# Attention and a gated MLP on one core: where one batch's token combinations are made, and the order of GpSimd's steps in the gate phase

## Chip, core and metric

The kernel runs on one core of one Trainium2 chip. Its five engines are named as in the profile: PE (TensorE, with PEld for its weight loads), DVE (VectorE), ACT (ScalarE), POOL (GpSimd) and SP (SyncE, which here only issues DMAs). Each engine works through its own queue in order. The metric is the time of one execution on the device in microseconds (us); the time of a kernel is the median of its runs.

## What is computed

For 8 batches, 8 heads, 576 tokens and a head width of 64, a Nystrom attention with 32 landmarks, and on its output a gated MLP. Cut to what matters:

```python
A, Bm, C = sm(q, k_lm), sm(q_lm, k_lm), sm(q_lm, k)   # sm: scaled, softmax
Z = Bm.T / (norm1(Bm) * norminf(Bm))
for _ in range(6):
    Z = 2 * Z - Z @ Bm @ Z
x = (A @ Z @ C @ v)                 # [8*576 tokens, 512]
xn = x / rms(x) * rms_g
g, val = xn @ w_gate, xn @ w_val    # 512 -> 1536
out = (silu(g) * val) @ w_out       # 1536 -> 512, float32
```

## The kernel before

A batch's attention output is not written out as x. The kernel keeps AT, the transposed attention weights in front of the last small product, scaled by the norm, as an operand `an` of 2 x 128 rows and 576 tokens, split in a high and a low part; the small product is multiplied into the MLP's gate and value weights instead (matmuls `pM`, "mixing"). All large products run as three matmuls: high by high, high by low, low by high.

The hidden width of 1536 lies in twelve blocks f of 128, in six pairs. The **first pass** does pairs 0 to 2 for all batches: `mlp(early, b, ...)` (L470) mixes a pair's weights (`mix_weights`, DVE low part L281), makes `psg` and `psv` (gate and value), the silu on ACT (L503), the product by `psv` on DVE (L504, which also frees that bank), splits it (h, L509), and `outs` (L512) multiplies by the output weights into `pso`, five or four groups of 128 tokens per batch, two at a time. `keep` (L1102) copies each group on ACT to `ob` (L1104) and writes it to DRAM as a partial result `pd`. Interleaved with it runs the attention of the batches to come (`steady`, `rest(b)` L729, `second(b)` L932): transposes L663, Newton steps (L874 to L890), the scaling, and at its end the token combinations below. A mixer places this work by estimated times. Raw weights (`wraw`, later `lraw`) are loaded and split by ACT and DVE (L180 to L195) as they are needed.

The **second pass**, the gate phase `seven(b)` (L373) and its `outs` for each batch, does pairs 3 to 5 with seven block products in place of eight. It reads the batch's operand and its combinations from DRAM (`ad` to `xb`). The combinations t1 to t4 are made in the first pass by `token_blocks` (L994): a subtraction on DVE (`less`, L1000), an ACT cast (L1004), a low part on DVE (L1005) and two DMAs per combination (L1007). Three t tiles go round. Weight combinations are made by `mix_blocks` (L295): matmuls `pM` into two PSUM banks, sums S7 on DVE (L320 to L331), casts Bhi on ACT (L314 to L339), low parts on DVE, and the largest, Blo, on POOL (L344).

Per block f, `step(f, n)` issues product n as three matmuls `p` of 288 columns, and what belongs to it: copies u of a bank (ACT L425, DVE L429), sums vv (L432, L451) and s (L409), silu (L405 and in step 6), multiplies (DVE L412; `gate1`, POOL L406), and `split`: the cast h (ACT L416) and its low part (POOL L418). Two blocks' steps are woven: (f,1), (f-1,5), (f,2), (f,7), (f,6), (f-1,3), (f-1,4).

All these instructions stay in the order of the program text on their engines (`kept`). PSUM has four banks in a pool `pg` (psg, psv, pso, and some pM and p) and four in `pm`. The s tiles of the gate phase and S7 share a ring of four buffers, u and vv have two each.

Batch 0 differs: its combinations are made in `rest(1)`, one step of `token_blocks` behind each of batch 1's Newton steps, and its third pair (pair 5) is mixed in pieces by `between` within `seven(0)`, while the other batches have all three pairs mixed in the output stage before:

```python
next(blocks_of[b - 1], None)                  # rest(b), after each newton_step
def between(b, f):                            # called by seven(b, ...)
    if b == 0 and f == 1:
        pieces.append(mix_blocks(0, NPAIR + 2, (pg, "pg"), False))
```

Of the kernel before, what the change touches and what calls it, by code (L numbers as in the profile page):

```python
# [9 lines left out]
F32 = mybir.dt.float32  # L10
# [45 lines left out]
def nystrom_moe_kernel(  # L56
# [238 lines left out]
    def mix_blocks(b, pair, banks, whole_pair=True):  # L295

        ps = mixed_banks(late, b, pair, banks)

        def sums(whole=True):
            homes = HOMES[pair % NPAIR]  # L300
            hi = wp.tile([P, 7, 2, P], F32R, name="Bhi", tag=homes[0])
            if (b, pair) == (0, NPAIR + 1):
                lo1, lo2 = (mp.tile([P, n, 2, P], F32R, name=f"Blo{n}", tag="wraw", bufs=RAWS) for n in (3, 4))
            else:
                lo = wp.tile([P, 7, 2, P], F32R, name="Blo", tag=homes[1])
                lo1, lo2 = lo[:, :3], lo[:, 3:]
# [4 lines left out]
            blocks7[b, pair] = hi, lo1, lo2  # L311

            def high(n):
                kept(nc.scalar.copy(hi[:, n], (a11, a12, a22)[n]))  # L314

            def low(n):
                kept(nc.vector.tensor_sub(lo1[:, n], (a11, a12, a22)[n], hi[:, n].bitcast(F32)))

            kept(nc.scalar.copy(s[:, 2], a21))
            kept(nc.vector.tensor_add(s[:, 0], s[:, 2], a22))  # L320
            yield
            high(0)
            kept(nc.vector.tensor_sub(s[:, 1], s[:, 0], a11))
            yield
            kept(nc.vector.tensor_sub(s[:, 2], a11, s[:, 2]))
            if whole:
                kept(nc.scalar.copy(hi[:, 1:3], both[1]))
            else:
                high(1)
            yield  # L330
            kept(nc.vector.tensor_sub(s[:, 3], a12, s[:, 1]))  # L331
            if not whole:
                high(2)
            yield
            low(0)
            for n in (slice(0, 4),) if whole else (slice(0, 2), slice(2, 4)):
                if n.start:
                    yield
                kept(nc.scalar.copy(hi[:, 3 + n.start : 3 + n.stop], s[:, n]))  # L339
                if not whole:  # L340
                    low(1 + n.start // 2)
            if whole:
                kept(nc.vector.tensor_sub(lo1[:, 1:3], both[1], hi[:, 1:3].bitcast(F32)))
            silu["mix"] = kept(nc.gpsimd.tensor_sub(lo2, s, hi[:, 3:].bitcast(F32)))  # L344

        def at_once():
            for _ in sums():
                pass

        return at_once if whole_pair else sums(False)  # L350
# [13 lines left out]
    later, pieces = [], []  # L364
# [8 lines left out]
    def seven(b, xb, between):  # L373
# [4 lines left out]
        def product(f, n, ps, first):  # L378
            hi, lo1, lo2 = own[f]
            at, of = PRODUCTS[n]  # L380
            hi = hi[:, at, f % 2]
            lo = lo1[:, at, f % 2] if at < 3 else lo2[:, at - 3, f % 2]
# [19 lines left out]
        def gate1(f):  # L402
            s = ss[f]
            eng = nc.gpsimd if f < NF1 - 1 else nc.vector
            silu["last"] = kept(nc.scalar.activation(s[:, 1], banks[f][0], AF.Silu))  # L405
            kept(eng.tensor_mul(s[:, 1], s[:, 1], vv[f][:, 1]))  # L406
# [4 lines left out]
        def gate0(f):  # L411
            kept(nc.vector.tensor_mul(ss[f][:, 0], ss[f][:, 0], vv[f][:, 0]))  # L412

        def split(f):
            s, h = ss[f].rearrange("p e s -> p (e s)"), hs[f]
            kept(nc.scalar.copy(h[:, 0, TAIL:], s))  # L416
            eng = nc.gpsimd if f < NF1 - 1 else nc.vector
            kept(eng.tensor_sub(h[:, 1, TAIL:], s, h[:, 0, TAIL:].bitcast(F32)))  # L418

        def step(f, n):  # L420
# [3 lines left out]
            if n == 1:  # L424
                kept(nc.scalar.copy(u[:, 0], p1))  # L425
                if f > 1:
                    gate1(f - 2)
            elif n == 5:
                kept(nc.vector.tensor_copy(u[:, 2], p1))  # L429
                if f == 0:  # L430
                    first0(1)
                kept(nc.vector.tensor_add(v_[:, 1], u[:, 2], p7))  # L432
                if last:
                    gate1(f - 1)
                    gate0(f - 1)
                    split(f - 1)
            elif n == 2:
                if f != 1:
                    first0(f)
                if f > 1:  # L440
                    gate0(f - 2)
            elif n == 6:
                kept(nc.scalar.copy(u[:, 1], p1))
                kept(nc.scalar.activation(s[:, 0], s[:, 0], AF.Silu))
                if f > 1:
                    split(f - 2)
            elif n == 3:
                if last:
                    gate1(f)
            elif n == 4:  # L450
                kept(nc.vector.tensor_add(v_[:, 0], u[:, 1], p7))  # L451
                if last:
                    gate0(f)
                    split(f)
# [3 lines left out]
        for f in range(NF1):  # L458
            yield from between(f)
            new(f)  # L460
            second = ((1, 5), (0, 2)) if f > 1 else ((0, 2), (1, 5))
            for d, n in ((0, 1), *second, (0, 7), (0, 6), (1, 3), (1, 4)):
                if f >= d:
                    yield from step(f - d, n)
                if pieces and n in (7, 4):
                    next(pieces[0], None)
# [3 lines left out]
    def mlp(wts, b, f0, an, store, part, following):  # L470
# [39 lines left out]
        yield from outs(wts, b, f0, store, part, following, NF1 - 1)  # L510
# [37 lines left out]
    with tc.tile_pool(name="ap", bufs=1, side="right") as ap, tc.tile_pool(  # L548
# [180 lines left out]
        def rest(b, inverse, at):  # L729
# [27 lines left out]
            for n in range(6):  # L757
# [3 lines left out]
                next(blocks_of[b - 1], None)  # L761
# [13 lines left out]
            if b == B - 1:  # L775
                for _ in blocks_of[b]:
                    yield -0.3
# [154 lines left out]
        def second(b):  # L932
# [56 lines left out]
            blocks_of[b] = token_blocks(b, ATs, to)  # L989
            ans[b] = an  # L990

        blocks_of = {}

# [201 lines left out]
    def between(b, f):  # L1195
        if b == 0 and f == 1:
            pieces.append(mix_blocks(0, NPAIR + 2, (pg, "pg"), False))
            yield 1.1

    mix.fill(mlp(early, B - 1, 0, ans.pop(B - 1), keep, lambda t: None, first_blocks))  # L1200
    for b in range(B):
        mix.fill(seven(b, nxt["xb"], lambda f, b=b: between(b, f)))
# [41 lines left out]
```

## Time and profile before

| | |
|---|---|
| time, median of 3 runs | 820.45 us (818.88 to 821.15) |
| the profiled execution, its own time | 819.86 us |
| its span, first to last instruction | 818.1 us |
| instructions | 18012 |
| mean granted clock of TensorE | 0.985 of 2.4 GHz |
| DMA | 109.7 MB, mean 134 GB/s |

PE's busy digits in 40 slices of 20.5 us; 9 is 90% or more of a slice:

```profile
PE   7876999999999999999999998899999999999997
PEclk9888999999999999999999999999999999999999
```

The first five digits cover the loads and the attention of the first batches. The first pass ends and the gate phase of batch 0 starts at about 495 us; each later batch takes about 37 to 41 us, of which some 17 are its gate phase and the rest its output stage.

### The profile page before, as it was taken

Reading aid. Unit: us, or ns where it says so; the run is one execution under the profiler, and the core shown is the slowest. Engines: PE = TensorE matmul, PEld = TensorE weight load, DVE = VectorE, ACT = ScalarE, POOL = GpSimd, SP = SyncE. Lnnn points to the kernel's source line nnn. Section 1 sums busy time; section 2 is a strip of 40 time slices with the busy share of each in tenths; the row PEclk is TensorE's granted clock in tenths of the full one; section 3 lists DMA queues with packets and bytes.
Section 4 is the critical chain, followed back from the end, with each engine's and each line's share of the span. In section 5 each row is a group of like instructions: output and inputs, shape, how many; then the busy total and the mean of one; then the engine's idle time right before and its main releaser. Section 6 shows DMA issues by size and latency. Waiting matters only on the chain.

```text
span 818.1 us, 18012 instructions
## 1 busy us (share of the span) xinstructions
PE 782.2 (96%) x7012; PEld 623.8 (76%) x7012; DVE 598.0 (73%) x1360; ACT 418.1 (51%) x925; POOL 226.4 (28%) x234
## 2 busy tenths in 40 slices
PE   7876999999999999999999998899999999999997
PEld 5554667877778778777787877697979797979796
DVE  7999898758878858678586875767576656766662
ACT  4467645435455445454474955455354444545450
POOL 1004311020110200200101042555355535544550
PEclk9888999999999999999999999999999999999999
DMA  9846554352450541621548521233332424151512
GB/s 326 283 152 232 167 191 143 103 169 73 133 175 23 189 153 58 198 75 58 169 148 273 163 77 39 102 104 135 96 115 91 153 78 147 58 179 53 175 30 77
DMA packets 54629, 109.70 MB, mean 134 GB/s; under 512 B 5392, under 2 KB 28944, under 8 KB 54544
## 3 DMA queue, kind: packets, MB, share of 16 engines
q1 hardware_dynamic: 54544, 108.55, 39.8%
q8 instruction: 55, 0.90, 0.5%
q14 instruction: 30, 0.25, 0.1%
HBM read 73.14 MB, written 35.39 MB: 133 GB/s over the span
## 4 chain that ended last, share of the span: by engine, by line
PE 83%; DVE 8%; issue 3%; ACT 2%; DMA 2%; POOL 1%; SPq 0%; DVEq 0%; POOLq 0%; ACTq 0%
PE pso L111 36%; PE p L111 14%; PE psg L111 9%; PE psv L111 9%; PE pM L111 5%; PE pn L111 2%; PE sC L111 2%; PE pCV L111 1%; PE pss L111 1%; PE pO L111 1%; DMA qk<-in_k_dram 1%; DMA vl<-in_vl_dram 1%; PE sE L117 1%; PE pW L111 1%; DVE u L429 0%
## 5 line engine op out<-in xcount | busy, mean ns | idle before, releaser
L111 PE MATMUL pso<-wo,h 128*128 128x512 f32 x648 | 158.5, 396 | 0.8 <-DVE s L504 0.8
L111 PEld LDWEIGHTS pso<-wo,h 128*128 128x128 f32 x648 | 118.6, 188 | 32.4 <-ACT E L616 4.2
L111 PE MATMUL p<-xb,Bhi 128*128 128x288 f32 x672 | 139.2, 301 | 4.1 <-DVE s L409 1.6
L111 PE MATMUL pso<-lhio,h 128*128 128x512 f32 x432 | 140.6, 394 | 0.9 <-ACT h L416 0.6
L111 PEld LDWEIGHTS p<-xb,Bhi 128*128 128x128 f32 x672 | 109.2, 190 | 12.1 <-ACT u L425 2.8
L111 PE MATMUL p<-xb,Blo 128*128 128x288 f32 x336 | 99.6, 296 | 2.3 <-POOL Blo L344 2.3
L111 PEld LDWEIGHTS pso<-lhio,h 128*128 128x128 f32 x432 | 81.0, 188 | 25.3 <-issue 5.9
L111 PE MATMUL psv<-an,Mhi 128*128 128x288 f32 x384 | 84.4, 304 | 4.8 <-DVE s L504 4.8
L111 PE MATMUL psg<-an,Mhi 128*128 128x288 f32 x384 | 85.7, 307 | 2.1 <-ACT an L983 1.2
L111 PE MATMUL pso<-lloo,h 128*128 128x512 f32 x216 | 84.3, 390 | 0.0
L111 PEld LDWEIGHTS psg<-an,Mhi 128*128 128x128 f32 x384 | 62.4, 191 | 14.1 <-DVE WT L890 5.0
L344 POOL TENSOR_TENSOR Blo<-S,Bhi 128x1024 fp32r<-128x1024 f32 x24 | 57.6, 2399 | 53.8 <-ACT Bhi L339 53.8
L418 POOL TENSOR_TENSOR h<-s,h 128x576 fp32r<-128x576 f32 x40 | 58.7, 1468 | 41.2 <-ACT h L416 41.2
L111 PEld LDWEIGHTS psv<-an,Mhi 128*128 128x128 f32 x384 | 62.8, 191 | 7.6 <-DVE s L504 5.3
L111 PEld LDWEIGHTS p<-xb,Blo 128*128 128x128 f32 x336 | 63.6, 189 | 2.5 <-POOL Blo L344 2.5
L649 POOL TENSOR_TENSOR tA<-tA,mA 128x576 f32<-128x576 f32 x16 | 18.8, 1194 | 169.0 <-DVE mA L648 169.0
L503 ACT ACTIVATE s<-psg 128x288 f32<-128x288 f32 x96 | 39.3, 410 | 42.0 <-PE psg L111 41.3
L111 PE MATMUL psv<-an,Mlo 128*128 128x288 f32 x192 | 59.0, 308 | 0.0
L111 PE MATMUL psg<-an,Mlo 128*128 128x288 f32 x192 | 58.6, 305 | 0.0
L416 ACT CAST h<-s 128x576 fp32r<-128x576 f32 x48 | 32.2, 672 | 50.8 <-POOL s L406 27.9
L1104 ACT COPY ob<-pso 128x512 f32<-128x512 f32 x36 | 21.0, 589 | 72.2 <-PE pso L111 44.8
L1165 DVE TENSOR_TENSOR obl<-obl,pso 128x512 f32<-128x512 f32 x36 | 24.6, 684 | 40.6 <-PE pso L111 40.5
(170 smaller groups left out, 1529.3 us busy)
## 6 DMA issues: line engine op xcount, KB each, us to landing
xb<-ad SPq DMA_DIRECT2D x16, 1008.0 KB, 6.0
qk<-in_q_dram SPq DMA_DIRECT2D x16, 576.0 KB, 4.5
qk<-in_k_dram SPq DMA_DIRECT2D x16, 576.0 KB, 6.2
ad<-t SPq DMA_DIRECT2D x64, 144.0 KB, 2.1
pd<-ob SPq DMA_DIRECT2D x36, 256.0 KB, 3.5
obl<-pd SPq DMA_DIRECT2D x36, 256.0 KB, 2.8
out_dram<-obl SPq DMA_DIRECT2D x36, 256.0 KB, 2.1
vt<-in_v_dram SPq DMA_DIRECT2D x16, 512.0 KB, 5.5
```

What stands on the lines that cost most here:

```text
L111: tc.keep_in_program_order(nc.tensor.matmul(*args, **kw))
L117: tc.keep_in_program_order(nc.tensor.transpose(*args))
L344: silu["mix"] = kept(nc.gpsimd.tensor_sub(lo2, s, hi[:, 3:].bitcast(F32)))
L416: kept(nc.scalar.copy(h[:, 0, TAIL:], s))
L418: kept(eng.tensor_sub(h[:, 1, TAIL:], s, h[:, 0, TAIL:].bitcast(F32)))
L503: silu["last"] = nc.scalar.activation(s[:, cols], banks[0], AF.Silu).ins
L649: nc.gpsimd.tensor_sub(tA, tA, mA.unsqueeze(2).broadcast_to([P, NB, M]))
L1104: nc.scalar.copy(ob, ps)
L1165: kept(nc.vector.tensor_add(ob, ob, ps))
```

## The change

Three things are done.

1. Batch 0's token combinations are no longer made in `rest(1)`. Its two AT tiles are written to a new DRAM buffer, `x_dram`, and `first_x` reads them back at the end of `rest(7)`, where the combinations of batch 7 and then of batch 0 are made.
2. Batch 0's third pair is mixed by `first_blocks`, in the output stage of the last first-pass batch, together with the other two, which now begins after 8 group steps of three matmuls rather than 12. All late weights are loaded first. `homes_of` finds buffers for the blocks; the low part on POOL is two instructions there. `between` and the pieces go.
3. In the gate phase the silu of half 1 is issued in step 3 of its own block; POOL's multiply (`times1`) of f-2 stays in step 1, and the cast and POOL's subtraction (`split`) move from step 6, of f-2, to step 1 of the next block, of f-3. In the last block the order differs as written.

```diff
-    def seven(b, xb, between):
+    def seven(b, xb):
...
         def gate1(f):
-            s = ss[f]
-            eng = nc.gpsimd if f < NF1 - 1 else nc.vector
-            silu["last"] = kept(nc.scalar.activation(s[:, 1], banks[f][0], AF.Silu))
-            kept(eng.tensor_mul(s[:, 1], s[:, 1], vv[f][:, 1]))
+            silu["last"] = kept(nc.scalar.activation(ss[f][:, 1], banks[f][0], AF.Silu))
+
+        def times1(f, eng):
+            kept(eng.tensor_mul(ss[f][:, 1], ss[f][:, 1], vv[f][:, 1]))
...
             if n == 1:
                 kept(nc.scalar.copy(u[:, 0], p1))
                 if f > 1:
-                    gate1(f - 2)
+                    times1(f - 2, nc.gpsimd)
+                if f > 2:
+                    split(f - 3, nc.gpsimd)
...
                 if last:
-                    gate1(f - 1)
-                    gate0(f - 1)
-                    split(f - 1)
+                    times0(f - 1)
+                    times1(f - 1, nc.gpsimd)
+                    split(f - 2, nc.gpsimd)
+                    split(f - 1, nc.gpsimd)
...
             elif n == 6:
                 kept(nc.scalar.copy(u[:, 1], p1))
                 kept(nc.scalar.activation(s[:, 0], s[:, 0], AF.Silu))
-                if f > 1:
-                    split(f - 2)
             elif n == 3:
+                gate1(f)
                 if last:
-                    gate1(f)
+                    times1(f, nc.vector)
...
-    def mlp(wts, b, f0, an, store, part, following):
+    def mlp(wts, b, f0, an, store, part, following, after=2 * NF1):
...
-                next(blocks_of[b - 1], None)
+                if b > 1:
+                    next(blocks_of[b - 1], None)
...
             if b == B - 1:
-                for _ in blocks_of[b]:
-                    yield -0.3
+                first_x()
+                for late_b in (b, 0):
+                    for _ in blocks_of[late_b]:
+                        yield -1.0
...
-            blocks_of[b] = token_blocks(b, ATs, to)
+            if b:
+                blocks_of[b] = token_blocks(b, ATs, to)
+            else:
+                for g in range(2):
+                    nc.sync.dma_start(x_dram[:, g * S : (g + 1) * S], ATs[g])
...
+        def first_x():
+            xs = [ap.tile([P, S], F32, name="x0", tag="E", bufs=2) for g in range(2)]
+            for g in range(2):
+                nc.sync.dma_start(xs[g], x_dram[:, g * S : (g + 1) * S])
+            blocks_of[0] = token_blocks(0, xs, a_dram[0].rearrange("p (a n s) -> p a n s", a=2, n=7))
...
     def first_blocks():
         nxt["xb"] = load_x(0)
+        while late.order:
+            late.load_next()
         first = mix_blocks(0, NPAIR, (pm, "pm"))
         later.append(mix_blocks(0, NPAIR + 1, (pm, "pm")))
+        later.append(mix_blocks(0, NPAIR + 2, (pg, "pg")))
         first()
-        yield 2.0
+        yield 2.9
...
-    mix.fill(mlp(early, B - 1, 0, ans.pop(B - 1), keep, lambda t: None, first_blocks))
+    mix.fill(mlp(early, B - 1, 0, ans.pop(B - 1), keep, lambda t: None, first_blocks, 8))
```

The mixer sets the order of the queues, so three places are shown as they stand on an engine, before and then with the change.

DVE in the first pass, beside batch 1's Newton steps (t is a combination of batch 0, w a weight being split, s<-s,psv the product that frees a bank). Before:

```order
L185 SCALAR_TENSOR_TENSOR w_1044<-w_1044,wrawo_920 128x512
L1000 TENSOR_TENSOR t_1070<-AT 128x288
L663 STREAM_TRANSPOSE AT<-tA 128x576
L188 SCALAR_TENSOR_TENSOR w_1044<-wrawo_920,w_1044 128x512
L1000 TENSOR_TENSOR t_1072<-AT 128x288
L504 TENSOR_TENSOR s<-s,psv 128x288
L281 TENSOR_TENSOR Mlo<-pM,Mhi 128x512 x2
```

With the change:

```order
L185 SCALAR_TENSOR_TENSOR w_1047<-w_1047,wrawo_923 128x512
L504 TENSOR_TENSOR s<-s,psv 128x288
L663 STREAM_TRANSPOSE AT<-tA 128x576
L188 SCALAR_TENSOR_TENSOR w_1047<-wrawo_923,w_1047 128x512
L879 SCALAR_TENSOR_TENSOR PV<-PV,pn 128x192
L281 TENSOR_TENSOR Mlo<-pM,Mhi 128x512 x2
```

The two t are gone, and L504 stands where the first of them stood, ahead of the transpose and the second weight instruction.

ACT in the output stage of the first pass's last batch (lhio a late weight; S, Bhi or B... the blocks of a mixed pair; ob the copy that frees a pso bank). Before:

```order
L194 CAST lhio_6485<-w_6480 128x512
L1104 COPY ob<-pso 128x512 x2
L319 COPY S_6540<-pM 128x256
L314 CAST Bhi<-pM 128x256
L327 CAST Bhi<-pM 128x512
L339 CAST Bhi<-S_6540 128x1024
L1104 COPY ob<-pso 128x512
```

With the change:

```order
L194 CAST lhio_6492<-w_6487 128x512
L341 COPY S_6539<-pM 128x256
L332 CAST Bwgv_6537<-pM 128x256
L332 CAST Bwgv_6537<-pM 128x512
L332 CAST Bwgv_6537<-S_6539 128x1024
L1118 COPY ob<-pso 128x512
L341 COPY S_6566<-pM 128x256
```

The first ob copies stood ahead of the first pair's copies; now the first ob stands behind all four of them.

POOL in the gate phase of batch 1 (s<-s,vv is the multiply of half 1, h<-s,h the low part). Before:

```order
L406 TENSOR_TENSOR s_7073<-s_7073,vv 128x288
L418 TENSOR_TENSOR h_744<-s_7073,h_744 128x576
L406 TENSOR_TENSOR s_7095<-s_7095,vv 128x288
L418 TENSOR_TENSOR h_886<-s_7095,h_886 128x576
L406 TENSOR_TENSOR s_7129<-s_7129,vv 128x288
```

With the change:

```order
L408 TENSOR_TENSOR s_7082<-s_7082,vv 128x288
L408 TENSOR_TENSOR s_7104<-s_7104,vv 128x288
L419 TENSOR_TENSOR h_747<-s_7082,h_747 128x576
L408 TENSOR_TENSOR s_7139<-s_7139,vv 128x288
L419 TENSOR_TENSOR h_889<-s_7104,h_889 128x576
L408 TENSOR_TENSOR s_7176<-s_7176,vv 128x288
```

A block's subtraction followed its own multiply; now the multiply of the next block stands between them.

## Rows read from the trace of the kernel before

**Rows 1.** busy time of each engine over the span (the page's part 1)

```profile
PE 782.2 (96%) x7012; PEld 623.8 (76%) x7012; DVE 598.0 (73%) x1360; ACT 418.1 (51%) x925; POOL 226.4 (28%) x234
```

**Rows 2.** windows: length, busy PE, PEld, DVE, ACT, POOL, PEclk, DMA, GB/s

```profile
494.70:519.53 24.83, 19.98 (x138) 17.73 (x136) 14.28 (x31) 12.47 (x32) 11.60 (x9) 0.93 0.03 12
...
539.68:556.50 16.82, 16.59 (x121) 16.01 (x120) 12.40 (x26) 9.70 (x25) 8.26 (x11) 1.00 0.21 64
```

**Rows 3.** PE's waits by releaser, 480 to 818 us: sum, count, longest

```profile
PE p L111 <- POOL Blo L344: 2.3, 1, 2.3
...
PE p L111 <- ACT u L425: 1.1, 7, 0.2
```

**Rows 4.** timeline, DVE and PE, first pass: start, us, instruction, [idle before <-releaser]

```profile
75.28 0.53 DVE L1000 TENSOR_TENSOR t<-AT 128x288 f32<-128x288 f32 x1
76.86 0.78 DVE L663 STREAM_TRANSPOSE AT<-tA 128x576 f32<-128x576 f32 x1 [1.05 <-POOL tA L661]
...
78.50 0.45 DVE L504 TENSOR_TENSOR s<-s,psv 128x288 f32<-128x288 f32 x1
79.00 0.61 PE L111 MATMUL psv<-an,Mhi 128*128 128x288 f32 x1 [4.38 <-DVE s L504]
```

**Rows 5.** windows, as in group 2, of the stretch behind that wait

```profile
80.00:90.00 10.00, 9.99 (x115) 8.07 (x108) 7.39 (x16) 5.34 (x10) 2.23 (x3) 0.78 0.43 143
```

**Rows 6.** chain that ended last: start, us, engine, tile, line, matmuls

```profile
472.36 8.18 PE pso L111 x36
...
525.95 2.74 PE pM L111 x48
...
539.85 2.80 PE p L111 x21
```

**Rows 7.** timeline of ACT, outputs of the first pass's last batch

```profile
482.88 0.62 ACT L194 CAST lhio<-w 128x512 fp32r<-128x512 f32 x1 [1.95 <-DVE w L188]
...
484.37 0.39 ACT L319 COPY S<-pM 128x256 f32<-128x256 f32 x1
...
486.43 1.05 ACT L339 CAST Bhi<-S 128x1024 fp32r<-128x1024 f32 x1 [0.60 <-DVE S L331]
```

**Rows 8.** costliest groups (part 5): busy, mean ns | idle before, releaser

```profile
L1104 ACT COPY ob<-pso 128x512 f32<-128x512 f32 x36 | 21.0, 589 | 72.2 <-PE pso L111 44.8
```

**Rows 9.** timelines of POOL and DVE in gate phases 0 and 1

```profile
512.52 2.35 POOL L344 TENSOR_TENSOR Blo<-S,Bhi 128x1024 fp32r<-128x1024 f32 x1
513.31 1.88 DVE L412 TENSOR_TENSOR s<-s,vv 128x288 f32<-128x288 f32 x1
...
547.98 1.43 POOL L418 TENSOR_TENSOR h<-s,h 128x576 fp32r<-128x576 f32 x1 [1.22 <-ACT h L416]
549.38 0.80 POOL L406 TENSOR_TENSOR s<-s,vv 128x288 f32<-128x288 f32 x1
549.48 1.01 DVE L412 TENSOR_TENSOR s<-s,vv 128x288 f32<-128x288 f32 x1
```

**Rows 10.** timelines of ACT and PE, end of gate phase 1

```profile
553.79 0.68 ACT L416 CAST h<-s 128x576 fp32r<-128x576 f32 x1 [0.74 <-POOL s L406]
...
554.81 0.53 PE L111 MATMUL p<-xb,Bhi 128*128 128x288 f32 x2 [0.16 <-ACT u L425]
```

**Rows 11.** timelines of DVE and PE, last batch

```profile
796.35 1.48 DVE L406 TENSOR_TENSOR s<-s,vv 128x288 f32<-128x288 f32 x1 [3.10 <-ACT s L405]
...
799.45 0.50 PE L111 MATMUL pso<-lhio,h 128*128 128x512 f32 x1 [0.65 <-ACT h L416]
```

**Rows 12.** timelines of SP, ACT, DVE near the first pass's end

```profile
446.10 0.38 SPq L157 DMA_DIRECT2D wrawg<-in_moe_w_gate_dram  x1
...
449.47 1.27 ACT L1104 COPY ob<-pso 128x512 f32<-128x512 f32 x2 [5.02 <-issue]
...
451.79 1.29 DVE L281 TENSOR_TENSOR Mlo<-pM,Mhi 128x512 fp32r<-128x512 f32 x2 [5.75 <-ACT Mhi L279]
...
462.36 0.67 ACT L180 ACTIVATE wrawg<-wrawg 128x512 int32<-128x512 uint32 x1
```

More of the change, by code (lines that the diff above doesn't have):

```diff
@@ L293, in nystrom_moe_kernel, with homes_of, four, within @@
     blocks7 = {}
-    def mix_blocks(b, pair, banks, whole_pair=True):
-        ps = mixed_banks(late, b, pair, banks)
[L299 to L306, printed above, removed]
+    def homes_of(b, pair):
+        def four(pool, tag, bufs, n=2):
+            return pool.tile([P, n, 2, P], F32R, name=f"B{tag}", tag=tag, bufs=bufs)
+        names = HOMES[pair % NPAIR]
+        if b or pair == NPAIR:
+            hi, lo = (four(wp, n, 1, 7) for n in names)
+            return [(0, hi)], [(0, lo)]
+        if pair == NPAIR + 1:
+            lows = [(0, four(mp, "wraw", RAWS, 3)), (3, four(mp, "wraw", RAWS, 4))]
+            return [(0, four(wp, names[0], 1, 7))], lows
+        first = four(mp, "w32", WB)
+        highs = [(0, first[:, :1]), (1, four(mp, "w32", WB)), (3, four(mp, "wraw", RAWS, 4))]
+        lows = [(0, first[:, 1:]), (1, four(lp, "obl", 4)), (3, four(mp, "s", 2)), (5, four(mp, "s", 2))]
+        return highs, lows
+    def within(parts, a, z):
+        for at, t in parts:
+            lo, hi = max(a, at), min(z, at + t.shape[1])
+            if lo < hi:
+                yield lo, hi, t[:, lo - at : hi - at]
+    def mix_blocks(b, pair, banks):
+        ps = mixed_banks(late, b, pair, banks)
+        def sums():
+            highs, lows = homes_of(b, pair)
             s = lq.tile([P, 4, 2, P], F32, name="S7", tag="lraw", bufs=4)
@@ L310, in sums, with high, low @@
             a12, a22 = both[1][:, 0], both[1][:, 1]
[L311 to L317, printed above, removed]
+            source = {0: both[0], 1: both[1], 3: s}
+            def high(n, z):
+                for a, e, to in within(highs, n, z):
+                    kept(nc.scalar.copy(to, source[n][:, a - n : e - n]))
+            def low(n, z, eng):
+                (_, _, h), = within(highs, n, z)
+                for a, e, to in within(lows, n, z):
+                    silu["mix"] = kept(
+                        eng.tensor_sub(to, source[n][:, a - n : e - n], h[:, a - n : e - n].bitcast(F32))
+                    )
             kept(nc.scalar.copy(s[:, 2], a21))
             kept(nc.vector.tensor_add(s[:, 0], s[:, 2], a22))
-            yield
-            high(0)
+            high(0, 1)
             kept(nc.vector.tensor_sub(s[:, 1], s[:, 0], a11))
-            yield
             kept(nc.vector.tensor_sub(s[:, 2], a11, s[:, 2]))
[L326 to L330, printed above, removed]
-            kept(nc.vector.tensor_sub(s[:, 3], a12, s[:, 1]))
[L332 to L350, printed above, removed]
+            high(1, 3)
+            kept(nc.vector.tensor_sub(s[:, 3], a12, s[:, 1]))
+            low(0, 1, nc.vector)
+            high(3, 7)
+            low(1, 3, nc.vector)
+            low(3, 7, nc.gpsimd)
+            blocks7[b, pair] = highs, lows
+        return sums
     def load_x(b):
@@ L362, in behind @@
         return tc.issue_after(ins) if ins else nullcontext()
-    later, pieces = [], []
+    later = []
     hs, ends = [], []
@@ L378, in product @@
         def product(f, n, ps, first):
-            hi, lo1, lo2 = own[f]
             at, of = PRODUCTS[n]
-            hi = hi[:, at, f % 2]
-            lo = lo1[:, at, f % 2] if at < 3 else lo2[:, at - 3, f % 2]
+            hi, lo = (next(within(parts, at, at + 1))[2][:, 0, f % 2] for parts in own[f])
             for k, (w, x) in enumerate(((hi, xb[0]), (hi, xb[1]), (lo, xb[0]))):
@@ L440, in step @@
                 if f > 1:
-                    gate0(f - 2)
+                    times0(f - 2)
             elif n == 6:
@@ L452, in step @@
                 if last:
-                    gate0(f)
-                    split(f)
+                    times0(f)
+                    split(f, nc.vector)
             yield 3 * MMG
@@ L458, in seven @@
         for f in range(NF1):
-            yield from between(f)
             new(f)
@@ L509, in mlp @@
                 gated[b, f0 // NF1, 2 * n + i] = nc.vector.tensor_sub(h[:, 1, TAIL:], s, h[:, 0, TAIL:].bitcast(F32))
-        yield from outs(wts, b, f0, store, part, following, NF1 - 1)
+        yield from outs(wts, b, f0, store, part, following, NF1 - 1, after)
     def outs(wts, b, f0, store, part, following, n0, after=2 * NF1):
@@ L1193, in next_blocks @@
             yield 2.9
[L1195 to L1198, printed above, removed]
-    mix.fill(mlp(early, B - 1, 0, ans.pop(B - 1), keep, lambda t: None, first_blocks))
+    mix.fill(mlp(early, B - 1, 0, ans.pop(B - 1), keep, lambda t: None, first_blocks, 8))
     for b in range(B):
-        mix.fill(seven(b, nxt["xb"], lambda f, b=b: between(b, f)))
+        mix.fill(seven(b, nxt["xb"]))
         mix.fill(outs(late, b, NF1, finish, load_part, lambda b=b: next_blocks(b), NF1 - 2, 2 * NF1 - 4))
```

8 lines of the change are left out of this document (3 added, 5 removed).

## The prediction, made before the changed kernel was run

> **What bounds the kernel now.** I read the busy times first, then the chain that ended last, then the waits of PE by releaser, and the stretches on it one by one. PE is busy for 782.2 of 818.1 us [rows 1], so an edit pays where it takes away an idle stretch of PE, a stretch at the lower clock, or PE's own work; the change adds and removes no PE work but for its place. The profiled execution took 819.86 us around a span of 818.1; the median of the runs is 820.45, 0.6 above it. A measurement of this kernel tells 0.3%, some 2.5 us, from no change.
>
> Three places of PE loss lie where the diff reaches. The gate phase of batch 0 takes 24.83 us and that of batch 1, of the same products, 16.82 [rows 2]; the largest single wait in the second pass lies there, 2.3 us for POOL's low part of a weight combination [rows 3]. In the first pass PE waits 4.38 us at 74.6 to 79.0 for one DVE product that frees a bank [rows 4]. And the other gate phases run a little above their own pace: 21 matmuls take 2.80 us [rows 6], so the 120 of a gate phase would take 16.0, and it takes 16.82.
>
> **Part 1, batch 0's combinations leave the first pass.** On DVE's queue the psv product of L504 starts at 78.50. Ahead of it stand a subtraction t at 75.28, a transpose that waited 1.05 for POOL, a weight instruction and a second t [rows 4]. The row order of the change puts L504 where the first t stood: 78.50 - 75.28 = 3.22 us earlier, and PE's wait falls from 4.38 to about 1.2. The waits for the transpose and for the weights stay; they now stand behind the product that PE waits for. The clock: in 80 to 90 the granted clock is 0.78 of 2.4 GHz, a part of the stretch at 1.2, though PE is busy for 9.99 of 10 us there [rows 5]; it fell after the idle stretch. That cost up to 0.22 x 10 = 2.2 us and may come back. Eight DVE instructions of about 0.45 us less (3.6 us) also leave this stretch, where DVE sits between PE's steps. I take 3.2 + 1.3 = **4.5**; from below 1.5 (half of the 3.2 goes into the next waits, and the clock falls all the same), from above 5.4 (3.2 + 2.2).
>
> The same 8 DVE instructions, 4 ACT casts and 8 writes of 144 KB come back near the end of the pass (at about 442 to 450 us), with 2 writes and 2 reads of 288 KB through DRAM new. DVE has 5.75 us free before 451.79 and ACT 5.02 before 449.47 [rows 12]; added are 8 x 0.45 = 3.6 on DVE and 4 x about 0.4 = 1.6 on ACT (the 256-column copy of [rows 7] takes 0.39). That fits, with a rest of 2 us for waits on the t writes, since three t tiles go round. On SP's queue the first half of batch 0's operands, xb, is now issued behind these 8 writes, and the weight load of 446.10 behind it; what it feeds starts on ACT at 462.36 [rows 12], 16 us later, so a delay of 8 us is covered. Without the cover the wait lands on PE's outputs pso. I take **-0.3**, between 0 and -2. The two reloads stand on SP ahead of the first late weight load and wait for the last reader of their tiles; that weight load has the same 16-us kind of slack, and I cost it at nothing.
>
> **Part 2, the third pair is mixed early.** Gate phase 0 should now go at the pace of the others: 24.83 - 16.82 = 8.01 us [rows 2]. Its 16 mixing matmuls pM still run, now in the output stage before: 16 of 48 at 2.74 [rows 6] = 0.91. Net **+7.1**. Bounds: 5 (something of the waits returns, the POOL part being due for the third pair) to 7.1. POOL has three low parts of 2.35 us to make instead of two; they start near 487 and the last is due at about 494.7 + 4 x 2.8 = 506, so they are covered.
>
> But these 16 pM need two banks of the pool that pso uses. In the output stage of the last first-pass batch the order on PE is now 24 pso, 48 pM, 12 pso, and then the third group of pso needs the bank of the first. PE reaches it at 472.36 + 24 x 8.18/36 + 2.74 + 12 x 8.18/36 = 483.3 [rows 6]. The bank comes free with the copy ob of the first group, which in the change's ACT order stands behind the last weight cast lhio and the four casts of the first mixed pair. The weight cast ends at 482.88 + 0.62 = 483.50, and before the four took from 484.37 to 486.43 + 1.05 = 487.48 [rows 7]; the ob copies that stood between are gone from there, so the four start at 483.5 and end 0.9 earlier, at 486.6; an ob takes 0.59 [rows 8]. PE gets the bank near 487.2: a **new stall of 3.9 us**, ended by ACT ob. After a stall of this size the clock went to 0.78 once [rows 5], so I add 0.8: **-4.7**. Bounds 0 (the copy is let through earlier, or PE has other work there) and -6.
>
> **Part 3, the order of the gate phase.** The multiply of half 1 and the subtraction for h go on POOL one after the other at step 1, and the silu on ACT comes earlier. In the gate phase the last break of PE is its wait for ACT u at 554.81; ACT's queue was held by the cast of h, which waited 0.74 us for POOL's multiply [rows 10]. Such waits for u number 7 in the second pass [rows 3], one a batch. In the new order that cast comes an iteration later, when POOL's multiply is done. A gate phase loses 16.82 - 16.0 = 0.8; I take half for this break: 7 x 0.41 = 2.9, and half of the 0.65 that PE waits for h in the last batch, behind a DVE product that waited 3.10 for ACT's silu [rows 11]: 0.3. **+3.2**; bounds -4 (a new wait of 0.5 in each of 8 batches) and +5.6 (7 x 0.8).
>
> A row speaks against this part. DVE's multiply L412, both inputs in SBUF, takes 1.88 us beside POOL's low part Blo and 1.01 beside POOL's multiply [rows 9], against 0.45 for such a product alone [rows 4]. POOL's multiply and subtraction are now back to back: 0.80 + 1.43 = 2.2 of every 2.8 us [rows 9], so L412 will more often meet one. DVE is busy 12.40 of 16.82 us in a gate phase [rows 2], 2.07 per 2.80, so a single added block of 0.7 is still covered. The Trainium skill, SBUF — State Buffer, "Who interferes with whom", has a rule: a DVE instruction with two SBUF inputs and a GpSimd instruction that reads SBUF share a port pair as an exclusive lock, and the loser blocks for the whole instruction. By that rule L412 could wait for a whole subtraction in each iteration, which is rival C; the 1.88 and 1.01 above agree with it.
>
> **Sum.** 4.5 - 0.3 + 7.1 - 4.7 + 3.2 = 9.8. 819.86 - 9.8 = 810.1, with the runs' median 0.6 above the profiled execution: 810.5.
>
> **The rivals.**
> - A, no stall in the output stage (the bank is freed in time): 4.7 more, **805.8**. For it: PE's queue and ACT's differ by a few us only. Against: the ACT order of the change, in which ob stands behind four casts.
> - B, the first-pass gain is small because the next wait takes its place, 1.5 rather than 4.5: **813.5**. For it: the transpose that waited for POOL is still there [rows 4]. Together with part 3 at nothing and 2 us lost to the late combinations it would be 813.5 + 3.2 - 0.3 + 2 = **818.4**; I hold the half of that (816) likelier than the whole.
> - C, DVE becomes the bound of the gate phase: L412 blocked for a whole subtraction of 1.43 [rows 9] in each iteration. 2.07 + 1.43 = 3.50 us against 2.80, 0.7 for each of 5 iterations in 8 batches = 28: **838.5**, slower than before. It decides when DVE's time per iteration passes 2.80, so from a block of 0.73. Against: the longest in the rows is 1.88, and that beside an instruction of 2.35 us [rows 9]; the blocks of today already are inside the 12.40.
> - D, the change does not do what it says in batch 0: waits for the operands or for POOL's low parts keep gate phase 0 at 24 us, and the new stall comes on top: 810.5 + 7 = **817.5** to 820.
>
> **How the numbers follow.** The forecast has 0.50, A 0.13, B 0.22 (0.14 at about 813.5, 0.08 at 816 to 818.4), C 0.07, D 0.08. The forecast's own terms move it between about 807 and 814. The range reaches from 804.5 (A with a little more of the clock) to 816.5 (B with most of its additions) and leaves out C, D and the end of B. Faster by over 0.3% is everything below 818.0: the forecast, A, most of B and half of D, 0.87; within it the rest of B and D, 0.06; slower is C, 0.07.
>
> **What would show it.** First pass: the psv after 74.6 starts near 75.8 and the clock in 80 to 90 is near 1.00. Output stage: PE idle some 4 us near 483 to 487, ended by ACT ob. Gate phase 0 takes 17 us and no wait for POOL's low part is left. Later gate phases take 16.4 and the waits for ACT u are gone. Wrong would be: gate phases of 17 us or more with DVE L412 near 1.9 each (C), no stall near 483 (A), or a wait of PE near 450 to 462 for weights or for ob.

## The result

The changed kernel takes 812.17 us (median of 4 runs, 811.62 to 813.13) against 820.07 before (4 runs, 818.88 to 821.15): a ratio of 0.9905 with a 95% interval of 0.9887 to 0.9924, 7.9 us less. The forecast was 810.5 with a range of 804.5 to 816.5, so the time lies inside. Its terms did not come out so well: the first pass gave more than I took, and the new order of the gate phase costs where I had it gain.

The page of the changed kernel, its part 1, answers to [rows 1]; the span fell by 8.2 us:

```profile
span 809.9 us, 18024 instructions
PE 777.5 (96%) x7012; PEld 618.7 (76%) x7012; DVE 612.5 (76%) x1359; ACT 418.6 (52%) x923; POOL 226.5 (28%) x235
```

PE was busy 4.7 us less with as many matmuls; its mean granted clock rose from 0.985 to 0.992. DVE was busy 14.5 us more though it lost an instruction: its multiply in the gate phases takes longer, as shown below.

PE's waits of the changed kernel, 470 to 810 us (us in total, times, longest), answer to [rows 3]: the wait for POOL's low part is gone, one for ACT ob is new, and the wait for ACT u, 1.1 in 7 times before, has grown.

```profile
PE pso L111 <- ACT ob L1118: 3.5, 1, 3.5
PE p L111 <- ACT u L426: 1.8, 8, 0.2
```

The windows of the changed kernel (columns as in group 2): gate phases 0 and 1, the stretch after the first-pass wait, and the outputs behind the new stall.

```profile
493.33:510.37 17.04, 16.75 (x121) 16.03 (x121) 12.50 (x24) 10.46 (x27) 7.63 (x7) 1.00 0.05 17
530.71:547.68 16.97, 16.68 (x121) 16.02 (x121) 13.19 (x25) 9.97 (x26) 8.37 (x11) 1.00 0.21 63
...
78.60:88.60 10.00, 9.91 (x117) 8.10 (x116) 8.89 (x18) 7.59 (x16) 3.96 (x5) 1.00 0.43 155
479.29:493.33 14.04, 14.04 (x56) 11.47 (x57) 4.84 (x12) 5.83 (x11) 6.87 (x4) 0.89 0.37 131
```

Against [rows 2], gate phase 0 fell from 24.83 to 17.04 and gate phase 1 rose from 16.82 to 16.97. Against [rows 5], the clock of the first-pass stretch is 1.00 in place of 0.78.

**Where the 8.2 us lie.** Three pieces of the chain that ended last stand in both traces at the same place of the program, and cut the span into stretches. Of the changed kernel:

```profile
424.69 8.18 PE pso L111 x36
...
530.71 2.80 PE p L111 x21
...
766.93 2.80 PE p L111 x21
```

The same pieces before start at 432.46, 539.85 and 775.01:

```profile
432.46 8.18 PE pso L111 x36
...
775.01 2.80 PE p L111 x21
```

The first matmul `pss` of batch 0 (the sums of squares for the norm) marks the end of the start-up; it began at 38.24 before and at 36.74 with the change. The differences of these starts, and of the spans, give the table; the experiments are cut in the same way.

| kernel | to pss | first pass | outputs and gate phase 0 | six batches | rest |
|---|---|---|---|---|---|
| before | 38.24 | 394.22 | 107.39 | 235.16 | 43.09 |
| changed | 36.74 | 387.95 | 106.02 | 236.22 | 42.97 |
| e1_gate_only | 37.22 | 393.28 | 107.77 | 236.05 | 42.88 |
| e2_old_gate | 36.74 | 388.21 | 105.90 | 235.00 | 43.15 |
| e3_combos_only | 36.79 | 388.49 | 108.75 | 234.96 | 43.11 |
| e4_pair_only | 37.56 | 393.62 | 105.86 | 234.84 | 43.02 |
| e5_ob_first | 36.52 | 388.09 | 101.85 | 236.11 | 43.03 |
| e6_ob_first_old_gate | 37.04 | 388.27 | 101.67 | 234.80 | 43.22 |
| e7_split_at6 | 37.06 | 388.05 | 106.17 | 235.98 | 43.14 |
| e8_ob_first_split_at6 | 37.44 | 387.91 | 101.81 | 235.98 | 43.16 |
| e9_one_multiply | 37.43 | 387.86 | 101.44 | 233.20 | 42.17 |
| e10_three_u | 37.33 | 388.92 | 101.19 | 232.77 | 42.19 |
| e11_write_only | 37.10 | 388.51 | 101.00 | 230.92 | 41.27 |
| e12_one_multiply_three_u | 37.02 | 387.95 | 101.69 | 235.10 | 42.84 |

Of the 8.2 us, 1.5 lie in the start-up, where no edit acts: kernels with the same instructions there show 36.5 to 38.2, and from 30 us to the pss the granted clock was 0.80 before and 1.00 with the change. I take this for chance of single executions; with one trace of each kernel it is not shown. The edits gave 6.27 in the first pass and 1.37 around gate phase 0, and lost 1.06 in six later batches.

### The profile page after: what moved, and what is told of

It is laid out like the page before. It is cut to its first block, busy times and chain, and to the rows that moved or that the text cites. A ratio compares the mean times of both kernels' runs of the same rounds, so it can differ in the third digit from the quotient of the medians.

```text
span 809.9 us, 18024 instructions
## 1 busy us (share of the span) xinstructions
PE 777.5 (96%) x7012; PEld 618.7 (76%) x7012; DVE 612.5 (76%) x1359; ACT 418.6 (52%) x923; POOL 226.5 (28%) x235
## 4 chain that ended last, share of the span: by engine, by line
PE 77%; DVE 13%; issue 3%; ACT 3%; DMA 2%; POOL 1%; SPq 0%; DVEq 0%; ACTq 0%; POOLq 0%
PE pso L111 35%; PE p L111 10%; PE psg L111 9%; PE psv L111 9%; PE pM L111 5%; DVE s L414 3%; PE pn L111 2%; PE sC L111 2%; PE pCV L111 1%; DVE s L411 1%; PE pO L111 1%; DVE u L432 1%; DVE lmT L572 1%; PE pss L111 1%; PE sE L117 1%
## 5 line engine op out<-in xcount | busy, mean ns | idle before, releaser
L111 PE MATMUL pso<-wo,h 128*128 128x512 f32 x648 | 160.2, 399 | 3.5 <-ACT ob L1118 3.5
L111 PE MATMUL p<-xb,Bwgv 128*128 128x288 f32 x560 | 92.1, 297 | 0.5
L111 PEld LDWEIGHTS p<-xb,Bwgv 128*128 128x128 f32 x560 | 81.3, 188 | 3.0 <-DVE vv L435 2.4
L111 PE MATMUL p<-xb,Bwo 128*128 128x288 f32 x392 | 74.2, 300 | 1.6 <-ACT u L426 1.6
L111 PEld LDWEIGHTS p<-xb,Bwo 128*128 128x128 f32 x392 | 58.8, 188 | 7.6 <-ACT u L426 4.6
L408 POOL TENSOR_TENSOR s<-s,vv 128x288 f32<-128x288 f32 x40 | 36.8, 919 | 75.0 <-ACT s L405 55.5
L414 DVE TENSOR_TENSOR s<-s,vv 128x288 f32<-128x288 f32 x48 | 55.6, 1159 | 0.3
```

The costliest lines, as they stand in the source:

```text
L111: tc.keep_in_program_order(nc.tensor.matmul(*args, **kw))
L408: kept(eng.tensor_mul(ss[f][:, 1], ss[f][:, 1], vv[f][:, 1]))
```

## The experiments

My theory after these traces: part 1 gives some 6 us, part 2 gives 7.8 at gate phase 0 and gives most of it back in the stall, part 3 costs 1 us because DVE's multiply is held up beside POOL's subtraction. The rivals are that the later batches lose for another reason, and that the stall belongs to the moved weight loads.

**Each part alone (e1 to e4).** e1_gate_only is the kernel before with part 3 of the diff alone, as quoted ahead of the prediction. Expected:

> The kernel before with the new gate-phase order alone (part 3). Theory: POOL's subtraction now meets DVE's two-SBUF multiply L414 and blocks it, so each later gate phase is about 0.15 us longer than before: DVE multiply near 1.15 mean instead of 0.72, PE waits of 0.23 for ACT u stay, time 0.5 to 1.5 us above before (about 821). Rival: the order gains what was predicted (0.4 a batch, waits for ACT u gone) and the changed kernel loses its microsecond in the later batches elsewhere: about 817.

Measured 819.5 (10 runs, 818.42 to 820.70), ratio 0.9997 (0.9985 to 1.0009): no difference that the runs tell, and the rise of 0.5 to 1.5 that I expected does not show in them. The traces are sharper: six batches take 236.05 against 235.16, 0.9 us more, and the rest 0.2 less. The rival's gain of 3 us is excluded. DVE's multiply in the later gate phases (busy, mean ns | idle before) is the one instruction of DVE whose mean changed; first before, then in e1:

```profile
L412 DVE TENSOR_TENSOR s<-s,vv 128x288 f32<-128x288 f32 x42 | 30.1, 717 | 0.2
...
L412 DVE TENSOR_TENSOR s<-s,vv 128x288 f32<-128x288 f32 x42 | 49.0, 1167 | 0.2
```

e2_old_gate is the reverse, the changed kernel with the old order, in its core:

```diff
-                    times1(f - 2, nc.gpsimd)
-                if f > 2:
-                    split(f - 3, nc.gpsimd)
+                    gate1(f - 2)
...
+                if f > 1:
+                    split(f - 2)
```

> The changed kernel with the old gate-phase order (parts 1 and 2 only). Theory: about 1 us faster than the changed kernel, 811.2, with batch periods as in the kernel before (41.2 and 37.5 us) and the DVE multiply at 0.72. Rival: 3 us slower than the changed kernel, 815.

Measured 811.10 (810.78 to 811.17), 1.1 below the changed kernel; six batches take 235.00. The loss in the later batches comes with part 3 and goes with it: in the table every trace of the old order takes 234.8 to 235.2 for the six batches, and changed, e1, e5, e7 and e8, which have the early silu, take 236.0 to 236.2.

e3_combos_only puts part 1 alone on the kernel before (`x_dram`, `first_x`, and `if b > 1` in `rest`).

> The kernel before with part 1 alone (batch 0's combinations made at the end of the first pass). Theory: PE is 6 us ahead of before by 112 us (3.2 from the bank's wait, the rest from the clock behind it and from later waits of the same stretch) and keeps it: about 814. Rival: only the wait's 3.2 us are the change's, and the rest is chance of the start-up: 816.5 or later. Second rival: the late combinations delay the end of the pass by 1 us or more, seen as a new wait of PE between 430 and 495 us.

Measured 813.71 (812.91 to 814.69), ratio 0.9923 (0.9900 to 0.9945). The first pass takes 388.49 and keeps it. Between the 36 pso of the table and those of the last first-pass batch lie 465.17 - 425.28 = 39.89 us, before 472.36 - 432.46 = 39.90: the late combinations cost nothing.

```profile
425.28 8.18 PE pso L111 x36
...
465.17 8.18 PE pso L111 x36
```

e4_pair_only puts part 2 alone on the kernel before (`homes_of`, `first_blocks` with the third pair, `after` of 8, no `between`).

> The kernel before with part 2 alone (third pair mixed early, old gate order, combinations in the first pass). Theory: gate phase 0 is 7.8 us shorter, the output stage ahead of it 0.9 longer by pM and has a stall of 3.5 us that ends with ACT ob, with near 2 us at the lower clock behind it: net 1 to 2 us faster than before, about 818.7. Rival: the stall is made by the shift of the weight loads in part 1 and is absent here: about 813.

Measured 816.98 (10 runs, 816.43 to 818.59), ratio 0.9965 (0.9955 to 0.9976): 3 us faster, where the stretch of the table gives 1.5. The stall is there without part 1, so the rival falls:

```profile
PE pso L111 <- ACT ob L1102: 3.5, 1, 3.5
```

**The stall (e5, e6).** In e5_ob_first the sums of the first pair are issued behind the store of the first output group:

```diff
         later.append(mix_blocks(0, NPAIR + 2, (pg, "pg")))
-        first()
+        later.insert(0, first)
         yield 2.9
```

> The changed kernel with the first pair's sums issued behind the first ob copy of the last first-pass batch. Theory: the stall of 3.55 us is made by that copy standing behind the four casts, and the 1.6 us of lower clock behind it come from the stall: PE waits at most 0.6 there, the 54 pso after it take 12.5 instead of 14.0, and the time is 4.5 us below the changed kernel, 807.6. Rival: the blocks of the three pairs come later by as much, and gate phase 0 waits for POOL's low parts instead: about 811 to 812.

Measured 807.47 (807.23 to 809.34), 4.7 below the changed kernel. In the changed kernel's timelines of ACT and PE (start, us, instruction, idle before and releaser) the first ob stands last, and PE starts when it is done; this answers to [rows 7]:

```profile
475.13 0.62 ACT L194 CAST lhio<-w 128x512 fp32r<-128x512 f32 x1 [1.95 <-DVE w L188]
475.66 0.37 ACT L341 COPY S<-pM 128x256 f32<-128x256 f32 x1
...
477.70 1.04 ACT L332 CAST Bwgv<-S 128x1024 fp32r<-128x1024 f32 x1 [0.60 <-DVE S L347]
478.66 0.58 ACT L1118 COPY ob<-pso 128x512 f32<-128x512 f32 x1
...
479.29 2.93 PE L111 MATMUL pso<-wo,h 128*128 128x512 f32 x6 [3.55 <-ACT ob L1118]
```

In e5_ob_first the ob follows the weight cast at once and PE waits 0.55; in the window behind it the clock is 1.00 where it was 0.89. The timelines:

```profile
475.05 0.62 ACT L194 CAST lhio<-w 128x512 fp32r<-128x512 f32 x1 [1.95 <-DVE w L188]
475.58 0.58 ACT L1118 COPY ob<-pso 128x512 f32<-128x512 f32 x1
...
476.21 0.96 PE L111 MATMUL pso<-wo,h 128*128 128x512 f32 x3 [0.55 <-ACT ob L1118]
```

and the window of its next 56 pso:

```profile
476.21:489.08 12.87, 12.83 (x56) 10.32 (x57) 7.35 (x18) 7.83 (x15) 6.89 (x5) 1.00 0.34 115
```

So the order on ACT makes the stall, and without the stall the clock did not fall: 3.55 - 0.55 = 3.0 us of waiting and 14.04 - 12.87 = 1.2 in the pace of the pso behind it are the 4.2 by which the stretch of the table shrank. Gate phase 0 did not come to wait for POOL.

e6_ob_first_old_gate adds the old gate order of e2_old_gate.

> The kernel of e5_ob_first with the old gate-phase order too. Theory: the losses of the stall and of the new gate order add, so 1 us below e5_ob_first: about 806.6. Rival: the new gate order only costs what chance of the start-up shows, and the two are equal within 0.3 us; the batch periods tell it (41.2 and 37.1 against 41.4 and 37.3 us).

Measured 807.34 (806.37 to 808.37): equal to e5_ob_first within the runs, where 1 us was expected. Its trace has the 1.3 us in the six batches (234.80 against 236.11), less 0.2 at the end and 0.5 of a later start-up; the runs alone don't settle it. Of three pairs that differ in part 3 alone (before and e1, e2 and changed, e6 and e5), all traces show its loss of 0.9 to 1.3 in the six batches, and the runs of one pair do, by 1.1.

**Why the gate order costs (e7 to e12).** One block of the changed kernel's gate phase 1, in the timelines of POOL, DVE, ACT and PE:

```profile
543.15 1.43 POOL L419 TENSOR_TENSOR h<-s,h 128x576 fp32r<-128x576 f32 x1 [0.86 <-ACT h L418]
543.20 1.70 DVE L414 TENSOR_TENSOR s<-s,vv 128x288 f32<-128x288 f32 x1
...
544.82 0.44 DVE L454 TENSOR_TENSOR vv<-u,p 128x288 f32<-128x288 f32 x1
...
545.38 0.40 ACT L426 COPY u<-p 128x288 f32<-128x288 f32 x1 [1.08 <-DVE vv L454]
...
545.83 0.40 PE L111 MATMUL p<-xb,Bwo 128*128 128x288 f32 x1 [0.23 <-ACT u L426]
```

DVE's multiply starts 0.05 us after POOL's subtraction and takes 1.70, near the 1.43 of the subtraction and its own 0.45 after it. DVE's next sum vv is late by as much, ACT's copy u waits 1.08 for vv, and PE waits for u. Over the 42 such copies of the later batches ACT's idle time that vv ended rose from 6.7 us before to 19.4 with the change:

```profile
L425 ACT COPY u<-p 128x288 f32<-128x288 f32 x42 | 16.6, 395 | 44.6 <-PE p L111 37.6 <-DVE vv L451 6.7
...
L426 ACT COPY u<-p 128x288 f32<-128x288 f32 x42 | 16.7, 399 | 57.9 <-PE p L111 38.5 <-DVE vv L454 19.4
```

e7_split_at6 moves the subtraction away, on the changed kernel:

```diff
             if n == 1:
...
                 if f > 1:
                     times1(f - 2, nc.gpsimd)
-                if f > 2:
-                    split(f - 3, nc.gpsimd)
...
                     times1(f - 1, nc.gpsimd)
-                    split(f - 2, nc.gpsimd)
                     split(f - 1, nc.gpsimd)
...
             elif n == 6:
...
+                if f > 1:
+                    split(f - 2, nc.gpsimd)
```

> The changed kernel with the cast of h and POOL's subtraction back at step 6 of f-2, the silu kept early. Theory: what blocks DVE's multiply L414 is the subtraction issued at step 1 beside it; moved away, the multiply falls from 1.16 to 0.75 mean or less, and since the silu is early the cast no longer waits for POOL, so the waits for ACT u (0.23 each) go below 0.1: gate phase 16.5, time 2 to 4 us below the changed kernel, 808 to 810. Rival: the early silu itself shifts ACT's copies u, and the gate phase stays at 17.0: 812.

Measured 812.61 (811.77 to 813.17): the rival. The multiply's mean fell to 827 ns, yet the six batches take 235.98. In its ACT timeline the cast of h waits for POOL's multiply again, and now the early silu too stands ahead of u, for which PE waits 1.7 us in 9 times after 490 us:

```profile
545.21 0.67 ACT L418 CAST h<-s 128x576 fp32r<-128x576 f32 x1 [0.42 <-POOL s L408]
545.79 0.40 ACT L405 ACTIVATE s<-p 128x288 f32<-128x288 f32 x1
546.10 0.39 ACT L426 COPY u<-p 128x288 f32<-128x288 f32 x1
```

So u can be late by ACT's order as well as by DVE, and the two orders only trade one for the other. e8_ob_first_split_at6 has the edits of e5 and e7.

> The kernels of e5_ob_first and e7_split_at6 together. Theory: both gains add: about 804 to 805.5. Rival: the ring of buffers or DVE becomes the limit when both are in, and the gain is only that of e5_ob_first: 807.6.

Measured 808.09 (807.89 to 808.32): the gain of e5_ob_first alone, as e7 lets one think.

e11_write_only tests, on e5_ob_first, whether it is POOL's reading that holds up the multiply:

```diff
-            kept(eng.tensor_sub(h[:, 1, TAIL:], s, h[:, 0, TAIL:].bitcast(F32)))
+            if eng is nc.gpsimd:
+                for _ in range(2):
+                    kept(eng.memset(h[:, 1, TAIL:].bitcast(F32), 0.0))
+            else:
+                kept(eng.tensor_sub(h[:, 1, TAIL:], s, h[:, 0, TAIL:].bitcast(F32)))
```

> The kernel of e5_ob_first with POOL's subtraction replaced by two writes of zeros over the same tile: the low part of h is left out for blocks 0 to 4 of each gate phase. Theory: DVE's multiply L414 is blocked by POOL instructions that read SBUF; beside writes alone it stays near 0.45, its mean falls from 1.16 to 0.7 or less (the multiply on POOL is left), and PE's waits for ACT u fall below 0.1. Rival: POOL's being busy at all, or the order of L414 among its neighbours, makes it long: the mean stays above 1.0.

One run, 800.62. POOL is still busy with 70 writes, and the multiply takes its own time:

```profile
L414 DVE TENSOR_TENSOR s<-s,vv 128x288 f32<-128x288 f32 x42 | 19.0, 453 | 0.2
...
L421 POOL MEMSET h<- 128x576 f32 x70 | 40.1, 579 | 2.0
...
535.29 1.22 POOL L421 MEMSET h<- 128x576 f32 x2
536.25 0.45 DVE L414 TENSOR_TENSOR s<-s,vv 128x288 f32<-128x288 f32 x1
```

The writes start earlier than the subtraction did, and in this block the multiply meets only their last 0.26 us; held up until they end, at 536.51, it would have taken some 0.7, an estimate from these two rows, and it took 0.45. The waits for u are gone and six batches take 230.92, 5.2 less than in e5_ob_first. So it is POOL's reading, not its being busy, that makes the multiply long. The Trainium skill, SBUF — State Buffer, "Who interferes with whom", says that a DVE instruction with two SBUF inputs contends with a GpSimd instruction that reads SBUF and not with one that only writes it; 1.70 us beside the subtraction and 453 ns beside the writes agree.

e9_one_multiply takes POOL's multiply away, on e5_ob_first:

```diff
+        def times(f):
+            kept(nc.vector.tensor_mul(ss[f], ss[f], vv[f]))
...
             if n == 1:
...
-                if f > 1:
-                    times1(f - 2, nc.gpsimd)
-                if f > 2:
-                    split(f - 3, nc.gpsimd)
...
                 if f > 1:
-                    times0(f - 2)
+                    times(f - 2)
...
             elif n == 6:
...
+                if f > 1:
+                    split(f - 2, nc.gpsimd)
```

> The kernel of e5_ob_first, both halves multiplied in one DVE instruction of 576 columns at step 2, and cast and POOL's subtraction at step 6 of f-2. POOL's multiply is gone from blocks 0 to 4, so the subtraction is over before the next DVE multiply. Theory: that multiply takes 0.8 (no block) in place of 1.16 + POOL's 0.92, the cast no longer waits, and PE's waits for ACT u fall below 0.1 each: 2 to 4 us below e5_ob_first, 803.5 to 805.5. Rival: ACT's order (cast and silu ahead of u, as in e7_split_at6) holds u back by itself: 807 or more.

Measured 803.85 (803.67 to 803.89), ratio to the kernel before 0.9804 (0.9787 to 0.9822), 3.6 below e5_ob_first. The multiply of 576 columns takes 1034 ns, not the 0.8 expected, but the trace's list of PE's waits has none for u any more.

```profile
L417 DVE TENSOR_TENSOR s<-s,vv 128x576 f32<-128x576 f32 x35 | 36.2, 1034 | 0.0
```

e10_three_u keeps the changed gate order of e5_ob_first and has a third buffer for u:

```diff
-            us[f] = mp.tile([P, 3, HS], F32, name="u", tag="Mhi", bufs=2)
+            us[f] = (lp.tile([P, 3, HS], F32, name="u", tag="u3", bufs=1) if f % 3 == 2
+                     else mp.tile([P, 3, HS], F32, name="u", tag="Mhi", bufs=2))
```

> The kernel of e5_ob_first with three buffers for u in place of two. Theory: ACT's copy u of a block waits for DVE's sum vv of the block two before because it takes that block's u buffer; with a third this wait goes, but a blocked DVE still reaches PE by the banks, so 0.1 to 0.3 us a gate phase come back: 805.5 to 807. Rival: the wait moves to DVE vv in full, and the time stays at 807.5.

Measured 803.55 (803.14 to 804.14), ratio 0.9802 (0.9787 to 0.9818): 3.9 below e5_ob_first, where I had given it 0.5 to 2. The multiply still takes 953 ns on average and PE no longer feels it. Its chain runs 90 products without a break, 12.20 us where e9 needs 12.56:

```profile
531.50 12.20 PE p L111 x90
...
552.80 15.52 PE pso L111 x66
```

So the wait for u was a wait for its buffer: the block lengthens DVE's work, and only the ring of two hands that on to PE.

e12_one_multiply_three_u has both edits.

> The kernels of e9_one_multiply and e10_three_u together. Theory: e9 still ran its 90 matmuls p in 12.6 us where e10 ran them in 12.19, and e10 lost 0.37 us a batch in the output stage, where e9 did not; with both, 12.2 and the shorter output stage: 0.43 x 8 = 3.4 us below e9_one_multiply, about 800.5. Rival: with POOL's multiply on DVE the sum vv is late for the banks all the same, and it stays between 802.5 and 804.

Measured 806.69 (5 runs, 806.35 to 808.18): slower than either, and neither theory gave it. Its 90 products take 12.57, as in e9. ACT's queue there has the cast, the silu and u back to back, without a wait (540.11 to 541.38), so I take ACT's order for the limit of both, which a buffer more doesn't help; no run moves that order alone. And its outputs are slower than in e9:

```profile
530.73 12.57 PE p L111 x90
...
552.38 15.52 PE pso L111 x66
```

Of e9_one_multiply the same pieces, with 15.22 for 66 pso:

```profile
530.87 12.56 PE p L111 x90
...
552.44 15.22 PE pso L111 x66
```

## Why the prediction held, and where it did not

**Part 1 was too small in its size: 4.5 forecast, 6.3 measured in the profiled pair, 5.5 as the mean of the three first passes with the old place of the combinations (393.7) less that of the others (388.2).** The step went as written: L504 starts at 73.87 and PE waits 1.16, of the forecast 1.2.

```profile
73.87 0.43 DVE L504 TENSOR_TENSOR s<-s,psv 128x288 f32<-128x288 f32 x1
...
74.36 0.40 PE L111 MATMUL psv<-an,Mhi 128*128 128x288 f32 x1 [1.16 <-DVE s L504]
```

The term was mis-sized twice. I counted 1.3 us for the clock, and 1.8 came back: the work from 79.00 to 84.23, at a granted clock of 0.50, took 5.23 us before, and the same work with the change 3.99, of which 0.56 is a new wait (columns as in group 2; first before, then with the change).

```profile
79.00:84.23 5.23, 5.23 (x44) 4.15 (x45) 3.46 (x8) 1.83 (x4) 1.21 (x1) 0.50 0.47 157
...
74.36:78.35 3.99, 3.36 (x45) 2.45 (x45) 3.11 (x7) 1.24 (x3) 1.87 (x2) 1.00 0.21 25
```

And two more waits of PE for L504 lay in the stretch, which I had read past; before, the waits from 60 to 113 us contain

```profile
PE psv L111 <- DVE s L504: 4.8, 2, 4.4
...
PE pso L111 <- DVE s L504: 0.8, 1, 0.8
```

which are 5.6 us for the one releaser, and 1.2 with the change. New waits of 0.6, 0.7 and 0.3 us (for the attention tiles PV, sqT and sq) took 1.6 of that back: 4.4 - 1.6 + 1.8 = 4.6. The other 1.7 of the profiled pair's 6.3 I can't place. The two other kernels with the old code (e1, e4) have a longest wait of 3.6 and 3.7 there rather than 4.4 and are 0.6 to 0.9 faster in the first pass, so a part of it is that execution's.

**The late combinations: -0.3 forecast, 0.0 measured** (e3). No new wait shows, so the room on DVE and ACT [rows 12] was enough.

**Part 2 was right in its mechanism and near in its sizes.** Gate phase 0 fell by 7.8 us where 8.0 was forecast, and mixing costs what was worked out. The stall came at the place, by the releaser and at the size written down, 3.55 against 3.9; the clock behind it cost more than the 0.8 that I took: the 54 pso took 14.04 us, against 12.87 in e5 and 12.46 before. Net +2.4 forecast, 1.4 in the profiled pair and 1.5 from before to e4. From e3 to e2 it is 2.9: in e3 the longest wait of gate phase 0 was followed by the lower clock, which cost 1.5 us there and did not happen before (the last section has the rows). So the profiled pair shows the least of what part 2 is worth.

**Part 3 failed: +3.2 forecast, -0.9 measured.** The step that failed is "in the new order that cast comes an iteration later, when POOL's multiply is done", from which I took half of the gate phase's loss. The cast no longer waited; but u is released by the later of two, ACT's queue and the buffer that DVE's vv frees, and the new order made the second later. Rival C was the right mechanism with the wrong price. It put 0.7 us on PE in each of five blocks. In gate phase 1 the multiplies take 1.28, 1.70, 1.70 and 1.38, which is 0.8 to 1.25 over the 0.45 of one alone, and DVE's period reaches 546.47 - 543.20 = 3.27 us by the starts of L414 in two blocks. But PE's 90 products took only 0.16 more, 12.91 (534.77 to 547.68) against 12.75 before (543.91 to 556.66), since the rings of buffers take up the first delays. The gain itself was to be had: without the wait for the buffer they take 12.20 in e10. The view that I should have followed one step further is the chain behind [rows 10]: I stopped at the first releaser of u and did not ask what is late next.

So the sum, 9.8 against 7.9 of the medians, came near by terms that failed in both directions: 1.0 to 1.8 too little in part 1, 0.3 of loss that did not come, and 4.1 too much in part 3; part 2 was between 1.0 too much and 0.5 too little. That the time lies so near the forecast is in part luck.

## What to carry to other kernels

When a change moves an instruction past a wait, list every resource that the waiting instruction needs (its queue, its operand, its output buffer) and compute when each comes free in the new order; the last one decides. An instruction that frees a PSUM bank belongs ahead of work that nobody waits for on its queue: one line moved took away 3.0 us of a 3.55-us stall and the lower clock behind it. And a DVE multiply with both inputs in SBUF is better kept away from POOL instructions that read SBUF, or given a buffer more to take up the delay: e9_one_multiply and e10_three_u, at 803.9 and 803.6, beat both kernels. The two together, in e12, do not add.

## What the runs showed of the hardware that I had not expected

In e10 and e12 every pso of the second pass is some 2% slower than in e9 and e5: 66 take 15.52 us in place of 15.22, 48 take 11.34 or 11.35 in place of 11.14, at the same count and a granted clock of 1.00 in the windows of all four, and the matmuls pso of the first pass take 8.18 for 36 in all of them. What the two kernels share is the third u buffer in the pool that also holds the late output weights and the loaded partial results, so these tiles may lie elsewhere in SBUF; no trace shows where they lie. Why PE is slower was not tried and stays open. By an estimate from these rows, 0.2 to 0.3 in each of eight batches, it hides some 2 us, without which e10_three_u would come near 801 to 802.

The clock fell to 1.2 GHz after some idle stretches and not after others of like length. In gate phase 0 with the old place of the third pair PE waits for POOL's low part, and the same matmuls follow: before, the wait was 2.29 us and they ran at a granted clock of 1.00; in e3_combos_only it was 2.02, and in e1_gate_only 1.84, and they ran at a mean of 0.73, in part at 1.2 GHz. The windows (columns as in group 2) of before, e3 and e1:

```profile
514.93:519.69 4.76, 4.76 (x35) 4.76 (x36) 2.95 (x7) 2.76 (x7) 3.14 (x3) 1.00 0.00 0
...
507.56:513.87 6.31, 6.30 (x35) 6.31 (x36) 2.72 (x7) 3.15 (x8) 3.14 (x3) 0.73 0.00 0
...
511.83:518.13 6.30, 6.29 (x35) 6.30 (x36) 3.80 (x8) 3.25 (x9) 4.52 (x5) 0.73 0.00 0
```

Two traces can so differ by 1.5 us in a stretch whose instructions the edit leaves as they were, as e3's does. What decides it is open.
